# Attention plus MLP on one core: the last key tiles of the last set in two query halves, and three key tiles' values scaled in the first phase

## The chip, the core and the metric

The kernel runs on one core of a Trainium2 chip. The metric is device time in microseconds (us) of one execution, input and output transfers of the program included. Lower is better. In the texts TensorE is PE, ScalarE is ACT, VectorE is DVE, GpSimd is POOL and SyncE, which issues most of the DMAs, is SP.

## The reference

`x` has 2048 tokens of 512 features. After a layer norm, 32 heads of 16 features attend over all 2048 tokens; an MLP of width 1792 works on the same normalised tokens, normalised once more; both are added to `x`.

```python
x = A_x
xn = _layernorm(x, axis=-1)
return x + _A_ref(xn, A_wqkv, A_wo) + _B_ref(xn, B_w1, B_b1, B_w2, B_b2)
# _A_ref: q, k, v = split(x @ wqkv) into 32 heads of 16
#   p = softmax(q k^T * 16**-0.5);  return (p v) @ wo
# _B_ref: y = layernorm(x); h = gelu(y @ w1 + b1); return h @ w2 + b2
```

## The kernel before

**Tiling.** Queries come in 4 tiles of 512 (`QW`), heads in 8 sets of 4 (`HS`), keys in 16 tiles of 128. A set `g` (0 to 31, `g = 8 * query tile + head set`) has 16 key tiles times 4 heads = 64 units. A unit is one matmul of scores, 128 keys by 512 queries, into one of the 8 PSUM banks (`qk`, the matmul at L1054; four heads sit in four row groups of the array).

**Two ways to the exponential.** ACT takes most units: one instruction over 2 or 3 banks (`fex` in `build_tile`, L1237, 1024 or 1536 columns) writes weights into `p_sb`, which has 15 slots; a slot is free again after the value matmuls of its key tile (`pv`, L1072). DVE takes whole key tiles out of `KD` = (2, 5, 8, 11, 14) (`build_dve`, `dve_terms`): per head one conversion to int16 (L1319), then four adds per key tile (L1343) that make four shifted copies. Their bits, read as f16, are five terms of an approximated exponential, so such a key tile has five rounds of value matmuls, the last four with scaled copies of the values (`vs`). The denominators come from a column of ones in the values `va`. How many key tiles of `KD` go to DVE is settled while the order is made: a set whose other key tiles are used up gives the rest to ACT.

**Stages.** In the first phase sets 0 and 1 run while the tokens are normalised, transposed (`xnT`), and turned into keys (`kt`) and values (`va`). A value matmul for key tile k waits for the values of tile k and of tile k+1 (`deps` in `build_pv`). The key tiles in `VSE` get their four scaled copies straight from the PSUM bank of the value projection (`scaled`, L938); those of the others are made later from a projection that is done again. `XACT` says up to which group of four token tiles ACT copies half of the transposes out of PSUM. After that, sets 2 to 31 run one after the other, with the MLP (`build_mlp`, `build_down`) and the output projection (`build_out`) fitted in between.

**After a set.** `build_opost` copies the set's sums out of PSUM (`osb`, L1377), and takes the denominators through DRAM: save (`ldram`, L1379), load spread over the partitions (`lc`, L1381), reciprocal on DVE (L1384), save (`rdram`, L1386), broadcast to 128 partitions (`rlb`, 256 KB, L1389), product on DVE (L1391). All five DMAs are issued by SP, in one line with the loads of MLP weights (`w_r`) and tokens (`x_r`). There is one `rlb` buffer, so a broadcast waits for the product before it. For the last set `build_opost_last` does without DRAM: per half of the queries a transpose out of PSUM (L1418), reciprocal, product, transpose back, all on DVE. Then `build_final` multiplies by the last rows of `wo`, adds the sum kept so far (`acc`, by an fp32 matmul with an identity for output tiles 0 and 2, on DVE for 1 and 3) and stores.

**The order.** All engines run a fixed order, made when the program is built by a planner (`_Plan`): operations with assumed durations, dependencies and a priority (a due time) are placed one by one on the engine that is free first. `TOL` and `KEEP` say how far PE may prefer an operation of the kind it is at; `T0`, `NST`, `KG`, `HLO`, `DN0`, `OL0`, `RATE` and their like only shift due times, `RESL`, `OPEN` and `HOT` steer which operations may start. Where the plan finds PE without work it places fill matmuls of zeros (`fill`, L1630). On the chip every engine takes its instructions in this order, so one that waits holds up all behind it on its engine.

Of the kernel before, what the change touches and what calls it, by code (L numbers as in the profile page):

```python
# [11 lines left out]
ALU = mybir.AluOpType  # L12
# [10 lines left out]
P = 128  # L23
DH = 16
HS = 4
QW = 512
# [35 lines left out]
class _Plan:  # L62
# [9 lines left out]
    TOL = 0.075  # L72
    KEEP = 2.0
# [406 lines left out]
def kernel(  # L480
# [149 lines left out]
    T0, NST = 13.5, 11.75  # L630
    KG, R0, VSP, NFI = 16.0, 29.0, 500.0, 2
    OL0, OL1 = -0.35, 0.25
    PAIR1, EPR = 1, -15

    VSE = (5,)
    D1 = ((1, 8),)
    OUT0, OUT1 = 1.3, 0.3
    HLO, HHI, DN0, DN1 = 0.17, 0.36, 0.58, 0.11
    PAIR = 1
    VX = 3  # L640
    HLO0, HHI0 = 0.3, 0.12
    OUT, OPEN, RES, RESL, SLK, ALP = 3, 2, 36, 28, 55.0, 0.0
    KTP, QTP = 65.0, 85.0
    HOT = 2
    XACT = 2
    F2 = 300.0
    CHUNK = 4
    HOLD = 75.0
    RATE, QO, PO, AO, DO = 23.75, 50.0, 44.5, 40.0, 14.5
# [329 lines left out]
    n_a = {g: 0 for g in range(NG)}  # L979
    stream = {"u": 0, "g": 0, "tile": 0, "cur": None, "end": False}  # L980

    def take_unit():

        u = stream["u"]
        if u < NU2:
            stream["u"] = u + 1
            stream["g"] = 1 if u >= END0 else 0
            return first_units[u] + (T0 + (start[2] - T0) * u / NU2,)
        cur = stream["cur"]
        if not cur:  # L990
            g = max(stream["g"], 2)
            if not left_a[g] and not left_d[g]:
                if g == NG - 1:
                    stream["end"] = True
                    return None
                g += 1
            stream["g"] = g
            k = left_a[g].pop(0) if left_a[g] else left_d[g].pop()
            cur = stream["cur"] = [(g, k, j) for j in range(HS)]
        g, k, j = cur.pop(0)  # L1000
        n_a[g] += 1
        stream["u"] = u + 1
        return g, k, j, ts_(g, min(n_a[g] / (HS * 12), 1.0))

    def units_left(g):
        return HS * len(left_a[g]) + (len(stream["cur"] or ()) if stream["g"] == g else 0)
# [44 lines left out]
    def qk(bank, g, k, j):  # L1051
        qt, s = divmod(g, NS)
        lo = 32 * j
        I(nc.tensor.matmul(ps[:, bank, :], lhsT=kt[lo:lo + 32, s // 2, k * P:(k + 1) * P],  # L1054
                           rhs=qz[lo:lo + 32, (qt * NB + s // 2) % NQB, s % 2, :],
                           start=True, stop=True, tile_position=(lo, 0)))
# [6 lines left out]

    def pv(g, k, rows):

        qt, s = divmod(g, NS)
        for vals, wts in rows:
            pv_done[g] += 1
            end = g in all_built and pv_done[g] == pv_need[g]
            for j in range(HS):  # L1070
                h = 8 * (s // 2) + 2 * j + s % 2
                I(nc.tensor.matmul(ps[32 * j:32 * j + 32, o_bank[g], :], lhsT=vals[:, h * VS:h * VS + 32],  # L1072
                                   rhs=wts(j), start=pv_done[g] == 1, stop=end,
                                   tile_position=(0, 32 * j)))
        if g in o_open:
            o_open.remove(g)
        if not end:
            o_open.append(g)
# [120 lines left out]
    def build_tile():  # L1199
# [15 lines left out]
        def fqk():  # L1215
            dl_now[0] = dl
            for x, (g, k, j, _) in enumerate(us):
                qk(b0 + x, g, k, j)
            if i in rider:
                rides(i)  # L1220
            build_tile()
        deps = []
        for (g, k, j, _) in us:
            deps += qk_deps(g, k)
# [18 lines left out]
        for x, (g, k, j, _) in enumerate(us):  # L1243
            unit_exp[g, k, j] = e
            unit_slot[g, k, j] = s0 + x
            unit_seq[g, k, j] = seq0 + x
            if j == HS - 1:
                whole[g].append((k, us[0][3]))
                if len(whole[g]) == (PAIR if seq0 >= NU2 else PAIR1):
                    build_pv(g)  # L1250
# [5 lines left out]
    def whole_set(g):  # L1256
        if g not in all_built and not left_d[g] and (
                built[0] >= (END0, NU2)[g] if g < 2 else not left_a[g]
                and (g < stream["g"] or not stream["cur"])):
            finish(g)  # L1260

# [146 lines left out]
    def build_opost_last(g):  # L1408
# [4 lines left out]
        e0, e1, e2 = None, None, mk_ok  # L1413
        for hf in range(2):
            qs = slice(hf * QW // 2, (hf + 1) * QW // 2)
            cs = slice(hf * HC, (hf + 1) * HC)
            tav = ta[:, qs].rearrange("p (c r) -> p c r", r=32)
            e0 = add("DVE", 0.36, lambda qs=qs: I(nc.vector.transpose(  # L1418
                out=ta[:, qs], in_=ps[:, o_bank[g], qs])), pv_ops[g] + h_use + [e1], pr,
                rel=(o_done(g),) if hf else ())  # L1420

            def f1(qs=qs, cs=cs, tav=tav):
                I(nc.vector.reciprocal(out=rl_t[:, cs], in_=tav[:, :, DH]))
                I(nc.vector.tensor_tensor(out=on_t[:, cs], in0=tav,
                                          in1=rl_t[:, cs].unsqueeze(2).to_broadcast([P, HC, 32]),
                                          op=ALU.mult))
                I(nc.vector.transpose(out=ont[:, slot, qs],  # L1427
                                      in_=on_t[:, cs].rearrange("p c r -> p (c r)")))
            e1 = add("DVE", 0.95, f1, [e0] + list(ont_use.get(g - NON, ())), pr)
            on_last.append(e1)  # L1430

            def f2(cs=cs, tav=tav):
                I(nc.gpsimd.tensor_scalar(out=okl[:, 0, cs], in0=tav[:, :, DH], scalar1=L_MIN,
                                          scalar2=None, op0=ALU.is_ge))
                I(nc.gpsimd.tensor_scalar(out=okl[:, 1, cs], in0=tav[:, :, DH], scalar1=L_MAX,
                                          scalar2=None, op0=ALU.is_le))
                I(nc.gpsimd.tensor_tensor(out=okl[:, 0, cs], in0=okl[:, 0, cs], in1=okl[:, 1, cs],
                                          op=ALU.mult))
                I(nc.gpsimd.tensor_tensor(out=okall[:, cs], in0=okall[:, cs], in1=okl[:, 0, cs],
                                          op=ALU.mult))  # L1440
            e2 = add("POOL", 1.3, f2, [e0, e2], pr)
# [118 lines left out]
    def build_final():  # L1560
        ga, gb = NG - 2, NG - 1
        outs = []
        for c in range(TQ):
# [3 lines left out]
            pool = tailp if c else misc  # L1567
# [6 lines left out]
            def fa(key=key, c=c, cs=cs, pool=pool):  # L1574
                mm(ps[:, pool.bank(key), :], ont[:, ga % NON, cs],
                   wo_pad[:, (ga % NS) // 2, ga % 2, :], c % 2 == 1, False)
# [4 lines left out]
            acq = ((pool, key),) if c else ((one, key), (misc, key))  # L1581
            dep = [acc_op[c], mk_idf] + ([exp_prev[0]] if c else [])
            if c % 2 == 0:
# [5 lines left out]
            def fe(c=c, key=key, pool=pool):  # L1589
                if c % 2:  # L1590
# [4 lines left out]
            outs.append(add("DVE" if c % 2 else "ACT", dve(D), fe, [m, y_use[0]], pr,  # L1595
# [85 lines left out]
```

## Time and profile before

| | |
|---|---|
| four runs | 817.59, 817.98, 817.54, 814.90 us; median 817.57 |
| profiled execution | 817.47 us, span of its instructions 815.7 us, mean granted PE clock 0.995 |
| PE busy | 780.6 us (96%), 9887 matmuls |
| DVE busy | 751.3 us (92%) |
| ACT busy | 775.5 us (95%), of it 733.9 in 649 exponentials (L1237): 355 of 1024 columns at 1054 ns, 294 of 1536 at 1483 ns |
| DMA | 27.99 MB, mean 34 GB/s |

The span goes from the first to the last instruction; the profiled execution is 1.77 us longer than it. A line of the timeline gives the start, the length, the engine, the line of code, what is written from what, and in brackets the idle time of the engine before it with what ended it. Records of a matmul overlap those after it (0.39 us each; a group of four that share the array takes about 0.215 us from start to start).

### The profile page before, as it was taken

Reading aid. Unit: us, or ns where it says so; the run is one execution under the profiler, and the core shown is the slowest. Engines: PE = TensorE matmul, PEld = TensorE weight load, DVE = VectorE, ACT = ScalarE, POOL = GpSimd, SP = SyncE. Lnnn points to the kernel's source line nnn. Section 1 sums busy time; section 2 is a strip of 40 time slices with the busy share of each in tenths; the row PEclk is TensorE's granted clock in tenths of the full one; section 3 lists DMA queues with packets and bytes.
Section 4 is the critical chain, followed back from the end, with each engine's and each line's share of the span. In section 5 each row is a group of like instructions: output and inputs, shape, how many; then the busy total and the mean of one; then the engine's idle time right before and its main releaser. Section 6 shows DMA issues by size and latency. Waiting matters only on the chain. (4 is left out here: it accounts for less than half of the span.)

```text
span 815.7 us, 23268 instructions
## 1 busy us (share of the span) xinstructions
PE 780.6 (96%) x9887; PEld 260.8 (32%) x9888; DVE 751.3 (92%) x1304; ACT 775.5 (95%) x676; POOL 59.6 (7%) x165
## 2 busy tenths in 40 slices
PE   8899999999999999999999999899999999999997
PEld 3333332333332333333333333233332333333332
DVE  8959999997899999997999999799899999999885
ACT  6779999999999999999999999799999999999995
POOL 3300001001000000000000010000100110000001
PEclk9999999999999999999999999899999999999999
DMA  6300031101010011100002012100000101210000
GB/s 188 97 17 2 21 80 31 36 14 30 16 36 8 29 48 37 52 22 10 15 16 41 22 35 46 44 21 22 23 16 16 28 16 40 62 42 28 13 23 33
DMA packets 54798, 27.99 MB, mean 34 GB/s; under 512 B 40613, under 2 KB 50598, under 8 KB 54690
## 3 DMA queue, kind: packets, MB, share of 16 engines
q1 hardware_dynamic: 52818, 25.03, 11.3%
q8 instruction: 78, 1.28, 0.6%
q10 hardware_dynamic: 1872, 1.44, 0.6%
q14 instruction: 30, 0.25, 0.1%
HBM read 23.85 MB, written 2.61 MB: 32 GB/s over the span
## 5 line engine op out<-in xcount | busy, mean ns | idle before, releaser
L1237 ACT ACTIVATE p_sb<-ps 128x1024 bf16<-128x1024 f32 (+1 forms) x649 | 733.9, 1248 | 23.4 <-PE ps L1054 12.0
L1054 PE MATMUL ps<-qz,kt 32*128 32x512 bf16 x2048 | 311.7, 384 | 19.0 <-ACT p_sb L1237 6.5
L1319 DVE TENSOR_SCALAR x_sb<-ps 128x512 int16<-128x512 f32 x456 | 301.1, 680 | 22.3 <-PE ps L1054 20.7
L1343 DVE TENSOR_SCALAR tb_x<-x_sb 128x2048 int16<-128x2048 int16 x304 | 202.6, 680 | 1.8 <-PE ps L1072 1.2
L1054 PEld LDWEIGHTS <-kt 32*128 32x128 bf16 x2048 | 85.0, 91 | 276.9 <-issue 269.8
L1072 PE MATMUL ps<-p_sb,va 128*32 128x512 bf16 x1592 | 157.6, 390 | 0.3 <-DVE osb L1377 0.3
L1072 PE MATMUL ps<-tb_x,vs 128*32 128x512 f16 x1216 | 112.0, 383 | 1.1 <-DVE tb_x L1343 0.9
L1343 DVE TENSOR_SCALAR x_sb<-x_sb 128x2048 int16<-128x2048 int16 x152 | 103.5, 681 | 4.1 <-PE ps L1072 3.5
L1072 PEld LDWEIGHTS <-va 128*32 128x32 bf16 x2048 | 49.7, 93 | 107.6 <-issue 104.2
L1072 PEld LDWEIGHTS <-vs 128*32 128x32 bf16 x1824 | 50.4, 96 | 44.3 <-issue 23.9
L1398 POOL TENSOR_SCALAR okt<-lc 128x16 f32<-128x16 f32 x31 | 10.9, 352 | 701.8 <-DMA lc<-ldram 701.8
L597 PE MATMUL ps<-yT,w_r 128*32 128x512 bf16 x896 | 59.4, 385 | 1.6 <-DVE ht L1498 0.8
L1072 PE MATMUL ps<-x_sb,vs 128*32 128x512 f16 x608 | 59.8, 383 | 0.7 <-DVE x_sb L1343 0.6
L597 PE MATMUL ps<-w_sb,ht 128*32 128x512 bf16 x896 | 59.6, 380 | 0.0
L1072 PE MATMUL ps<-x_sb,va 128*32 128x512 f16 x456 | 45.0, 384 | 1.4 <-DVE x_sb L1319 1.2
L1498 DVE TENSOR_SCALAR ht<-ps,b_sb 128x512 bf16<-128x512 f32 x56 | 41.4, 739 | 2.3 <-PE ps L597 2.2
L1630 PE MATMUL ps<-ones_bf,zeros_bf 128*32 128x512 bf16 x416 | 36.8, 384 | 0.0
L597 PE MATMUL ps<-wo_pad,ont 128*32 128x512 bf16 x512 | 33.9, 380 | 0.5 <-DVE ont L1427 0.2
L597 PEld LDWEIGHTS <-w_r 128*32 128x32 bf16 x896 | 22.8, 96 | 26.1 <-issue 12.4
L597 PEld LDWEIGHTS <-ht 128*32 128x32 bf16 x896 | 21.7, 96 | 21.7 <-issue 5.7
L1508 ACT ACTIVATE ht<-ht 128x3584 bf16<-128x3584 bf16 x8 | 25.1, 3182 | 0.0
L1377 DVE COPY osb<-ps 128x512 f32<-128x512 f32 x31 | 21.1, 681 | 0.5 <-PE ps L1072 0.3
(100 smaller groups left out, 363.3 us busy)
## 6 DMA issues: line engine op xcount, KB each, us to landing
rlb<-rdram SPq DMA_DIRECT2D x31, 256.0 KB
w_r<-in_B_w_dram SPq DMA_DIRECT2D x56, 128.0 KB
x_r<-in_A_x_dram SPq DMA_DIRECT2D x16, 128.0 KB
w_sb<-in_B_w_dram SPq DMA_DIRECT2D x1, 1792.0 KB
out_dram<-ot SPq DMA_DIRECT2D x12, 128.0 KB
x_sb<-in_A_x_dram SPq DMA_DIRECT2D x2, 512.0 KB
wkv<-in_A_wqkv_dram ACTq DMA_DIRECT2D x1, 512.0 KB
x_sb<-in_A_x_dram ACTq DMA_DIRECT2D x1, 512.0 KB
```

The costliest lines, as they stand in the source:

```text
L597: I(nc.tensor.matmul(dst[32 * j:32 * j + 32], lhsT=lhsT[:, 32 * j:32 * j + 32], rhs=rhs, start=start, stop=stop, tile_position=(0, 32 * j)))
L1054: I(nc.tensor.matmul(ps[:, bank, :], lhsT=kt[lo:lo + 32, s // 2, k * P:(k + 1) * P], rhs=qz[lo:lo + 32, (qt * NB + s // 2) % NQB, s % 2, : ...
L1072: I(nc.tensor.matmul(ps[32 * j:32 * j + 32, o_bank[g], :], lhsT=vals[:, h * VS:h * VS + 32], rhs=wts(j), start=pv_done[g] == 1, stop=end, ...
L1237: I(nc.scalar.activation(p_sb[:, s0:s1, :].rearrange("p a b -> p (a b)"), ps[:, b0:b0 + n, :].rearrange("p a b -> p (a b)"), AF.Exp, scale ...
L1319: I(nc.vector.tensor_scalar(out=ib[sl][:, j, :], in0=ps[:, pool.bank(key), :], scalar1=LEVEL, scalar2=0.0, op0=ALU.add, op1=ALU.max))
L1343: I(nc.vector.tensor_scalar(out=tb[x].rearrange("p j q -> p (j q)"), in0=ib[sl].rearrange("p j q -> p (j q)"), scalar1=float(SHIFT[t]), sc ...
L1377: e0 = add("DVE", dve(QW), lambda: I(nc.vector.tensor_copy(osb[:, i2, :], ps[:, o_bank[g], :])), pvs + before, pr - 1000, rel=(o_done(g),))
L1398: I(nc.gpsimd.tensor_scalar(out=okt[:, 0, :], in0=lc[:, i2, :], scalar1=L_MIN, scalar2=None, op0=ALU.is_ge))
L1498: I(nc.vector.tensor_scalar(out=ht[:, fc, :], in0=ps[:, misc.bank(key), :], scalar1=b1_sb[:, fc:fc + 1], scalar2=None, op0=ALU.add))
L1508: I(nc.scalar.activation(out=hv, in_=hv, func=AF.Gelu_apprx_tanh, scale=1.0))
L1630: I(nc.tensor.matmul(ps[32 * j:32 * j + 32, o_bank[opened], :], lhsT=zeros_bf[:, 0:32], rhs=ones_bf[:], start=False, stop=False, tile_posi ...
```

## The change

1. **Last set in halves.** Of set 31, the last four key tiles that ACT takes (`NHK`), once DVE's key tiles are given out, are cut into half units: a unit now holds two key tiles for 256 queries. All half units of the first 256 queries come first, then those of the others. The first half goes into the set's bank, whose group is closed by a matmul of zeros; the second half goes into a bank of its own (`O2`), to which what the set's bank holds for these queries is added through a copy on DVE and an fp32 matmul with an identity.
2. **Post-processing by halves.** `build_last_half` does for one half what `build_opost_last` did in a loop, the first half as soon as its sums are complete. In `build_final` only output tile 2 takes `acc` by the fp32 matmul; tiles 0, 1 and 3 add it on DVE.
3. **Values.** `VSE` is (5, 8, 11) in place of (5,); `D1` is empty, so key tile 8 of set 1 goes to ACT; `XACT` is 3.
4. **Constants of the planner** are other ones, so the order changes everywhere.

```diff
-    TOL = 0.075
-    KEEP = 2.0
+    TOL = 0.05
+    KEEP = 1.0
...
-    T0, NST = 13.5, 11.75
-    KG, R0, VSP, NFI = 16.0, 29.0, 500.0, 2
-    OL0, OL1 = -0.35, 0.25
+    T0, NST = 14.0, 12.75
+    KG, R0, VSP, NFI = 14.75, 29.5, 450.0, 1
+    NHK = 4
+    OL0, OL1 = -0.95, 0.2
...
-    VSE = (5,)
-    D1 = ((1, 8),)
-    OUT0, OUT1 = 1.3, 0.3
-    HLO, HHI, DN0, DN1 = 0.17, 0.36, 0.58, 0.11
+    VSE = (5, 8, 11)
+    D1 = ()
+    OUT0, OUT1 = 1.075, 0.55
+    HLO, HHI, DN0, DN1 = 0.07, 0.42, 0.58, 0.05
     PAIR = 1
-    VX = 3
-    HLO0, HHI0 = 0.3, 0.12
-    OUT, OPEN, RES, RESL, SLK, ALP = 3, 2, 36, 28, 55.0, 0.0
-    KTP, QTP = 65.0, 85.0
-    HOT = 2
-    XACT = 2
-    F2 = 300.0
+    VX = 2
+    HLO0, HHI0 = 0.3, 0.135
+    OUT, OPEN, RES, RESL, SLK, ALP = 3, 2, 28, 30, 60.0, 25.0
+    KTP, QTP = 40.0, 85.0
+    HOT = 1
+    XACT = 3
+    F2 = 150.0
     CHUNK = 4
-    HOLD = 75.0
-    RATE, QO, PO, AO, DO = 23.75, 50.0, 44.5, 40.0, 14.5
+    HOLD = 0.0
+    RATE, QO, PO, AO, DO = 23.0, 70.0, 52.0, 32.5, 14.5
...
+            if g == NG - 1 and len(left_a[g]) <= NHK:
+
+                if not left_d[g]:
+                    halves.extend((ks, j, hf) for hf in range(2)
+                                  for ks in zip(left_a[g][::2], left_a[g][1::2])
+                                  for j in range(HS))
...
             dl_now[0] = dl
-            for x, (g, k, j, _) in enumerate(us):
-                qk(b0 + x, g, k, j)
+            for x, (g, k, j, _, *hf) in enumerate(us):
+                if not hf:
+                    qk(b0 + x, g, k, j)
+                for d in range(2 * len(hf)):
+                    qk(b0 + x, g, k[d], j, slice(d * QH, d * QH + QH),
+                       slice(hf[0] * QH, hf[0] * QH + QH))
...
+    def build_pv_half(g, ks, hf):
...
+            for d, k in enumerate(ks):
+                for j in range(HS):
+                    h = 8 * (s // 2) + 2 * j + s % 2
+                    I(nc.tensor.matmul(
+                        ps[32 * j:32 * j + 32, misc.bank("O2") if hf else o_bank[g], cs],
+                        lhsT=va[:, k, h * VS:h * VS + 32],
+                        rhs=p_sb[:, x[j][1], d * QH:d * QH + QH],
...
+            if not hf and complete(g):
+                for j in range(HS):
+                    I(nc.tensor.matmul(
+                        ps[32 * j:32 * j + 32, o_bank[g], :], lhsT=zeros_bf[:, 0:32],
+                        rhs=ones_bf[:], start=False, stop=True, tile_position=(0, 32 * j),
+                        skip_group_check=True))
...
+    def build_last_half(g, hf):
...
+        if hf == 0:
+            whole_o = pv_ops[g] + half_ops[0]
+            e0 = add("DVE", 0.45, lambda: I(nc.vector.transpose(
+                out=ta[:, qs], in_=ps[:, o_bank[g], qs])), whole_o + h_use, pr)
+            rest = slice(QH, QW)
+            c = add("DVE", 0.36, lambda: I(nc.vector.tensor_copy(
+                osb[:, g % 2, rest], ps[:, o_bank[g], rest])),
+                whole_o + [e0] + list(osb_use.get(g - 2, ())), pr, rel=(o_done(g),))
+
+            def fo():
+                half_left[1] -= 1
+                I(nc.tensor.matmul(ps[:, misc.bank("O2"), rest], lhsT=ident_f[:],
+                                   rhs=osb[:, g % 2, rest], start=False,
+                                   stop=half_left[1] == 0, skip_group_check=True))
+            half_ops[1].append(add("PE", 0.5, fo, [c, mk_idf], pr - 100, hold=1, mode="d"))
+        else:
+            e0 = add("DVE", 0.45, lambda: I(nc.vector.transpose(
+                out=ta[:, qs], in_=ps[:, misc.bank("O2"), qs])), half_ops[1] + [e1], pr,
+                rel=(misc.giver("O2"),))
...
-            pool = tailp if c else misc
+            pool = tailp if c > 1 else misc
...
-            if c % 2 == 0:
+            if c == 2:
                 dep = [add("PE", 0.9, fi, dep, pr - 20, acq=acq, mode="d")]
```

## The prediction

> **What bounds the kernel now.** First the busy shares of the page:
>
> ```profile
> PE 780.6 (96%) x9887; PEld 260.8 (32%) x9888; DVE 751.3 (92%) x1304; ACT 775.5 (95%) x676; POOL 59.6 (7%) x165
> ```
>
> PE and ACT look alike, so I asked for the waits of ACT by stretch. From 75 to 520 us it idles 4.3 us, from 540 to 804 us 1.6 us: there ACT is the bound, and what it is given or spared counts in full. Its other idle time lies in three places. In all:
>
> ```profile
> ACT p_sb L1237 <- PE ps L1054: 12.0, 30, 2.7
> ACT p_sb L1237 <- PE ps L1072: 8.0, 2, 4.5
> ```
>
> **Place one**, the first phase. The two waits for L1072 (value matmuls, which free slots of `p_sb`) are 3.48 us before 29.10 and 4.54 us before 49.32. ACT's timeline, then PE's:
>
> ```profile
> 41.01 3.77 ACT L1237 ACTIVATE p_sb<-ps 128x1024 bf16<-128x1024 f32 x4 [0.34 <-ACT p_sb L1237]
> 49.32 15.57 ACT L1237 ACTIVATE p_sb<-ps 128x1024 bf16<-128x1024 f32 x16 [4.54 <-PE ps L1072]
> ```
> ```profile
> 45.26 1.91 PE L597 MATMUL ps<-xnT,wkv 128*32 128x512 bf16 x32
> 47.10 1.91 PE L597 MATMUL ps<-wkv,xnT 128*32 128x512 bf16 x32
> 48.83 0.40 PE L1072 MATMUL ps<-p_sb,va 128*32 128x512 bf16 x4
> ```
>
> PE does 64 projection matmuls in one go before the value matmul (48.83) that frees the slots. That one needed the values of key tile 8, which DVE copies out at 48.20.
>
> **Place two**, 520 to 530 us. The windows (the column after POOL is the granted clock), the timeline, and the chain that ended last:
>
> ```profile
> 520.00:524.00 4.00, 1.90 (x23) 0.61 (x20) 1.75 (x4) 2.74 (x3) 1.30 (x4) 0.94 0.27 68
> 524.00:528.00 4.00, 3.92 (x33) 1.06 (x31) 3.31 (x6) 1.45 (x1) 0.00 (x0) 0.50 0.00 0
> 528.00:532.00 4.00, 4.00 (x49) 1.02 (x41) 2.70 (x5) 2.88 (x3) 0.00 (x0) 0.70 0.00 0
> ```
> ```profile
> 513.38 0.53 SPq L1389 DMA_DIRECT2D rlb<-rdram  x1
> 514.16 0.51 SPq L1379 DMA_DIRECT2D ldram<-osb  x1
> ...
> 522.25 0.25 DVE L1384 RECIPROCAL rc<-lc 128x16 f32<-128x16 f32 x1 [2.44 <-DMA lc<-ldram]
> ...
> 523.70 1.67 PE L1054 MATMUL ps<-qz,kt 32*128 32x512 bf16 x5 [2.10 <-DVE x_sb L1319]
> ...
> 525.48 1.45 ACT L1237 ACTIVATE p_sb<-ps 128x1536 bf16<-128x1536 f32 x1 [2.73 <-PE ps L1054]
> ```
> ```profile
> 514.16 4.50 DMA ldram<-osb
> 518.73 3.44 DMA lc<-ldram
> ```
>
> Set 18's broadcast of 256 KB goes out 0.78 us ahead of set 19's save. Save and load land after 8 us; in most sets POOL, which waits for the same load, starts 3.5 us after the copy. The reciprocal holds DVE for 2.44 us, PE runs dry for 2.10 us, its clock falls to half, and ACT loses 2.73 + 2.20 + 0.22 = 5.15 us.
>
> **Place three**, the tail. The last exponential ends at 805.41:
>
> ```profile
> 803.04 2.37 ACT L1237 ACTIVATE p_sb<-ps 128x1024 bf16<-128x1024 f32 x2 [0.23 <-PE ps L1054]
> ...
> 806.35 0.69 DVE L1553 TENSOR_TENSOR wkv<-ps,wkv 128x512 f32<-128x512 f32 x1 [1.47 <-PE ps L597]
> ...
> 806.96 0.44 DVE L1418 STREAM_TRANSPOSE ht<-ps 128x256 f32<-128x256 f32 x1
> ...
> 808.49 0.41 DVE L1418 STREAM_TRANSPOSE ht<-ps 128x256 f32<-128x256 f32 x1
> ...
> 810.13 0.62 PE L597 MATMUL ps<-wo_pad,ont 128*32 128x512 bf16 x8 [0.24 <-DVE ont L1427]
> ...
> 810.87 0.69 DVE L1591 TENSOR_TENSOR yT<-ps,wkv 128x512 bf16<-128x512 f32 x1
> ```
>
> Both halves' post-processing (1.59 us each) follows it in line; DVE ends at 811.56, 6.15 us after ACT. The 4.14 us from there to the end of the span are the store, the flag and the branch, which stay.
>
> **The change, part by part.** Counts are those of the built order; the sum is against the profiled execution, 817.47 us (0.10 under the median of the four runs).
>
> *More for ACT: +4.2 us.* Key tile 8 of set 1 goes to ACT (2 instructions of 1024 columns), and one more key tile does so in a later set (114 DVE key tiles become 112): 359 such instructions against 355, the 294 of 1536 stay. 4 x 1.05 = 4.2, on the path. The half units do not change ACT's columns. DVE loses 8 conversions and 8 adds, 16 x 0.68 = 11 us, and PE 10 - 2 = 8 rounds of value matmuls, 8 x 0.215 = 1.7 us: both have idle time already, so nothing.
>
> *First phase: -3.4 us.* Up to the score matmuls of unit 64, PE has 104 K and 176 V projection matmuls before, 40 and 192 after: 48 fewer, 12 groups of four x 0.215 = 2.6 us. Three groups of 16 transposes also come later (0.34 each, 1.0), and four changes between score and other matmuls go (0.32 from start to start for one group against 0.215, so 0.1 each, 0.4). PE is there 4.0 us earlier. The longest row of PE work without scores was 5.5 us here; after it is one projection (0.98) and one transposition. Key tile 8's copy stood behind four key copies, whose projections PE made first; now it follows that of tile 7 after two DVE instructions, and its projection is no longer late. The stall of 4.54 should go. Against it stand two PSUM copies that move to ACT (`XACT`; 2 x 0.588 = 1.18), in a stretch where PE and ACT are about level: I charge them in full, 4.54 - 1.18 = 3.4. Ends: 4.5 (copies hidden) and 1.2 (PE still late by half). The first stall has the same order of PE before it and stays. The eight scalings that come earlier (8 x 0.62 = 5.0 on DVE) fall where DVE has room: it is busy 11.2 us of the 20 from 40 to 60; without that cover they would cost 5.0. The two projections not made again (32 matmuls, 1.7 us of PE later on) are worth nothing where ACT is the bound.
>
> *Place two: -4.3 us.* All order changes, so this coincidence does too. In the new order, the DVE work between broadcast 18 and set 19's copy is 10.7 us; it was 0.6. If the event goes, ACT gets 5.15 us; at most the 1.6 us idle that ACT had later could have absorbed some of a delay, so 3.5 to 5.15; I take the middle. That the four runs hold one at 814.90, 2.6 below the others, fits a stall that does not always bite, but does not show it.
> The Trainium skill ("TensorE: Matmul & The Clock Gate", The HAM clock gate) has the clock fall after an idle window of about 3.4 us. Here 0.50 follows 2.10 us of idle, so the row decides. By the page's rule the loss would be the DVE wait alone, 2.4, and the forecast 814.0.
>
> *Tail: -1.9 us.* The first half's chain (1.59) and its carry into the second bank now stand before the last two half-unit value matmuls or beside them. From the last exponential: value matmuls 0.45 (0.06 to start, a group of 0.215, 0.17 to land), half two's chain 1.59, then on DVE three additions (0.65, 0.65, 0.69) and the reduction of 0.15 in line: 4.2 us against 6.15. PE's own line is shorter: 12 output matmuls 0.65, the fp32 identity 0.99 (1.98 for two in the trace), 16 more 0.86, ends at 3.0. Ends: 1.0, if the carry's fp32 matmul (256 columns, half of 0.99 = 0.5), which waits on DVE ahead of the last value matmuls in PE's line, comes late by a microsecond, or the last score matmuls, which stand behind twelve value matmuls of DVE's last terms, do; and 2.8, if only 0.45 + 1.59 + 0.62 + 0.69 = 3.35 counted.
> Score matmuls of 256 columns do not occur before; the nearest rows, 128 columns at 221 ns and 512 at 384, give for 16 more at most 16 x 0.38 = 6 us if each stood alone, and 0 if they share the array as their like do. PE has fills in this stretch, so I take 0.
> Against the change speaks "TensorEngine Tiling (Array Packing)", Instruction Overhead: some 60 cycles with each matmul. By that, the 32 more would cost an estimated 0.8 us of PE time, and the forecast would be 812.9.
>
> Sum: 4.2 - 3.4 - 4.3 - 1.9 = -5.4; 817.47 - 5.4 = **812.1 us**. With the ends of the terms taken partly together, 809.5 to 815.3. ACT's small waits elsewhere (5.9 us) may shift by 1 either way, inside that.
>
> **The rivals.** A difference of 0.3% (2.45 us, so 815.1 to 820.0) is about what a measurement here can tell.
>
> *One DMA wait takes the place of the old one: 816.4 to 817.3.* Counting DVE instructions at 0.61 us each (1.20 for two L1319 in the chain), a broadcast now goes out 0.6 to 1.8 us ahead of the next copy's end in six sets (1, 4, 5, 9, 24, 25), against two before (1 and 19, about 0.5). For it: number, and four loads of `wo` between set 4's save and load. Against: DVE work between copy and reciprocal is 6.1 us or more in five of them (4.8 in set 19, whose wait it was), and set 1, with a broadcast between save and load, had its data after 5.57 us, without a stall.
>
> *Two or more such waits, each with the clock drop: slower, 821.6 or more.* Same place; it decides once a load lands some 2 us after DVE has run out of work, as in set 19 (8.1 us). 812.1 + 4.3 + 5.15 = 821.6.
>
> *The first-phase saving fails: 816.6.* The added scalings hold one of the two PSUM banks of these projections for five DVE instructions each, and DVE is busy 19.46 us of the 20 from 20 to 40. If the stall comes back elsewhere, 812.1 + 4.54 = 816.6. Against: those of tile 8 come after the copies that the value matmuls wait for.
>
> **How the numbers follow.** Forecast 0.62 (nearly all under 815.1), one wait 0.17, no first-phase saving 0.10, two waits 0.11. Faster 0.61, same 0.27, slower 0.12. The range takes in the forecast's own 809.5 to 815.3 and the two middle cases with a microsecond above: 809 to 818.3; what it leaves out is the slower case and about 0.07 beside.
>
> **What would show it.** ACT without a stall of 4.5 us near 45 to 50, the one near 25 to 29 still there; 359 exponentials of 1024 columns; no window with a clock near 0.50 and no reciprocal with a wait over 1 us; DVE's last addition about 4.2 us after the last exponential, the first half's transpose before its end. Wrong, if ACT's idle time between 60 and 800 us grows beyond 8 us, if a reciprocal waits over 2 us for `lc`, or if the last exponential ends later than 804.

## The result, and the profile after

The changed kernel takes 818.91 us (median of 42 runs, 813.9 to 825.2 but for one disturbed run), the kernel before 816.72 (63 runs, 814.7 to 819.1): a ratio of 1.0028, 95% interval 1.0018 to 1.0039. The change makes the kernel slower by 0.28%, clear of noise but just under the 0.3% that the prediction took for what a measurement here can tell; it had forecast 812.1, a faster kernel. The profiled execution took 818.66 us, with a span of 816.9 and a mean granted clock of 0.990.

The busy shares and ACT's waits, from the page and the waits of the kernel after:

```profile
PE 776.5 (95%) x9823; PEld 257.6 (32%) x9824; DVE 741.8 (91%) x1288; ACT 779.5 (95%) x681; POOL 55.3 (7%) x165
```
```profile
ACT p_sb L1265 <- PE ps L1072: 13.3, 21, 6.1
ACT p_sb L1265 <- PE ps L1095: 4.3, 4, 3.8
```

PE and DVE have less to do, as predicted. ACT's longest wait is no longer one of 4.5 us for value matmuls (now L1095) but one of 6.1 us for score matmuls (now L1072). I added up ACT's time from the first to the last exponential in both traces, and what follows it:

| us | before | after | change | predicted |
|---|---|---|---|---|
| ACT busy | 770.1 | 774.7 | +4.6 | +4.2 + 1.2 |
| ACT idle up to 75 us | 9.7 | 4.9 | -4.8 | -4.5 |
| ACT idle behind 75 us | 13.9 | 16.0 | **+2.1** | **-4.3** |
| last exponential to DVE's end | 6.21 | 4.07 | -2.1 | -1.9 |
| DVE's end to the end of the span | 4.06 | 5.45 | **+1.4** | **0** |

Three of the five rows came as predicted; the two others turn -5.4 into +1.2.

**First phase.** ACT's timeline of the kernel after:

```profile
29.12 2.87 ACT L1265 ACTIVATE p_sb<-ps 128x1024 bf16<-128x1024 f32 x3 [3.77 <-PE ps L1095]
...
37.08 23.15 ACT L1265 ACTIVATE p_sb<-ps 128x1024 bf16<-128x1024 f32 x24
```

The first stall stands, the second, at 49 us, is gone: 24 exponentials follow one another.

**The new wait.** SyncE's issues around set 4's save, then the timeline of all engines, ACT's timeline, and the windows (the eighth figure of a window, after POOL's, is the granted clock):

```profile
149.66 0.82 SPq L665 DMA_DIRECT2D wo_pad<-in_A_wo_dram  x2
150.57 0.55 SPq L1468 DMA_DIRECT2D rlb<-rdram  x1
151.17 0.96 SPq L665 DMA_DIRECT2D wo_pad<-in_A_wo_dram  x2
152.18 0.51 SPq L1458 DMA_DIRECT2D ldram<-osb  x1
152.75 2.69 SPq L665 DMA_DIRECT2D wo_pad<-in_A_wo_dram  x4
159.85 0.36 SPq L1460 DMA_DIRECT2D lc<-ldram  x1
```
```profile
161.84 0.25 DVE L1463 RECIPROCAL rc<-lc 128x16 f32<-128x16 f32 x1 [3.52 <-DMA lc<-ldram]
...
162.70 0.58 PE L1072 MATMUL ps<-qz,kt 32*128 32x512 bf16 x1 [3.40 <-DVE x_sb L1398]
```
```profile
173.55 7.31 ACT L1265 ACTIVATE p_sb<-ps 128x1024 bf16<-128x1024 f32 x6 [6.12 <-PE ps L1072]
```
```profile
160.00:164.00 4.00, 1.30 (x6) 0.21 (x5) 2.15 (x5) 3.98 (x3) 0.92 (x4) 0.72 0.05 6
164.00:168.00 4.00, 4.00 (x27) 0.90 (x30) 2.97 (x5) 3.42 (x3) 0.00 (x0) 0.50 0.00 0
```

The broadcast of 256 KB (`rlb`) and eight loads of `wo` lie around the save, four of them between it and its load. SyncE waits until 159.85 for the save to land, 7.7 us after its issue. The reciprocal holds DVE for 3.52 us, PE runs dry for 3.40, the clock falls to half for 10.2 us, and ACT, which has other work until 167.4, loses 6.12 us before 173.55. This is place two of the kernel before again, larger, in set 4 instead of 19.

**The end.** The timeline of all engines, cut to DVE:

```profile
805.92 0.45 DVE L1502 STREAM_TRANSPOSE ht<-ps 128x256 f32<-128x256 f32 x1 [0.57 <-PE ps L1095]
...
807.88 0.45 DVE L1516 STREAM_TRANSPOSE ht<-ps 128x256 f32<-128x256 f32 x1 [0.16 <-PE ps L1314]
...
811.27 0.13 DVE L1552 CAST flag_i<-ps 1x1 int32<-1x1 f32 x1
```

The first half is transposed 1.4 us before the last exponential ends (807.34), and DVE ends 4.07 us behind it, as predicted. Then comes what no view of the profile lists, since branches do not count as busy; the trace has it. All engines read the flag and branch past the code that is not needed. PE's branch takes 3.28 us (812.53 to 815.81; before 0.41), one of SyncE's last waits stands behind it from 814.57 to 815.96, and the span ends 1.4 us later after DVE's end than before.

### The profile page after: what moved, and what is told of

Its sections match the earlier page's. It is cut to its first block, busy times and chain, and to the rows that moved or that the text cites. A ratio compares the mean times of both kernels' runs of the same rounds, so it can differ in the third digit from the quotient of the medians.

```text
span 816.9 us, 23106 instructions
## 1 busy us (share of the span) xinstructions
PE 776.5 (95%) x9823; PEld 257.6 (32%) x9824; DVE 741.8 (91%) x1288; ACT 779.5 (95%) x681; POOL 55.3 (7%) x165
## 4 chain that ended last, share of the span: by engine, by line
PE 29%; DVE 22%; ACT 8%; issue 4%; DMA 2%; DVEq 0%; SPq 0%; ACTq 0%
PE ps L1095 10%; DVE x_sb L1398 10%; PE ps L597 9%; PE ps L1072 9%; ACT p_sb L1265 7%; DVE tb_x L1422 5%; DVE x_sb L1422 3%; DMA ldram<-osb 1%; DVE ht L1601 1%; ACT ht L1611 1%; DVE osb L1456 1%; DMA lc<-ldram 1%; DVE qc L919 0%; DVE ont L1470 0%; PE ps L1733 0%
## 5 line engine op out<-in xcount | busy, mean ns | idle before, releaser
L1072 PE MATMUL ps<-qz,kt 32*128 32x512 bf16 (+1 forms) x2064 | 310.9, 381 | 21.4 <-DVE x_sb L1398 9.2
L1398 DVE TENSOR_SCALAR x_sb<-ps 128x512 int16<-128x512 f32 x448 | 296.1, 680 | 28.8 <-PE ps L1072 28.1
L1422 DVE TENSOR_SCALAR tb_x<-x_sb 128x2048 int16<-128x2048 int16 x299 | 199.4, 681 | 5.1 <-PE ps L1095 4.0
L1072 PEld LDWEIGHTS <-kt 32*128 32x128 bf16 x2064 | 83.4, 91 | 269.8 <-issue 262.6
L1095 PE MATMUL ps<-p_sb,va 128*32 128x512 bf16 x1584 | 157.5, 390 | 0.9 <-DVE x_sb L1398 0.7
L1095 PE MATMUL ps<-tb_x,vs 128*32 128x512 f16 x1196 | 110.8, 384 | 2.3 <-DVE tb_x L1422 1.8
L1422 DVE TENSOR_SCALAR x_sb<-x_sb 128x2048 int16<-128x2048 int16 x149 | 101.5, 681 | 1.9 <-PE ps L1095 1.6
L1095 PEld LDWEIGHTS <-va 128*32 128x32 bf16 x2032 | 48.5, 93 | 105.2 <-issue 102.6
L1095 PEld LDWEIGHTS <-vs 128*32 128x32 bf16 x1792 | 50.8, 96 | 52.4 <-issue 31.3
L1477 POOL TENSOR_SCALAR okt<-lc 128x16 f32<-128x16 f32 x31 | 14.5, 468 | 707.1 <-DMA lc<-ldram 707.1
L1095 PE MATMUL ps<-x_sb,vs 128*32 128x512 f16 x596 | 58.7, 383 | 1.5 <-DVE x_sb L1422 1.3
L1095 PE MATMUL ps<-x_sb,va 128*32 128x512 f16 x448 | 44.2, 384 | 0.9 <-DVE kt L901 0.5
L597 PEld LDWEIGHTS <-w_r 128*32 128x32 bf16 x896 | 21.7, 96 | 23.9 <-issue 10.2
```

What stands on the lines that cost most here:

```text
L597: I(nc.tensor.matmul(dst[32 * j:32 * j + 32], lhsT=lhsT[:, 32 * j:32 * j + 32], rhs=rhs, start=start, stop=stop, tile_position=(0, 32 * j)))
L1072: I(nc.tensor.matmul(ps[:, bank, to], lhsT=kt[lo:lo + 32, s // 2, k * P:(k + 1) * P], rhs=qz[lo:lo + 32, (qt * NB + s // 2) % NQB, s % 2, of],
L1398: I(nc.vector.tensor_scalar(out=ib[sl][:, j, :], in0=ps[:, pool.bank(key), :], scalar1=LEVEL, scalar2=0.0, op0=ALU.add, op1=ALU.max))
L1422: I(nc.vector.tensor_scalar(out=tb[x].rearrange("p j q -> p (j q)"), in0=ib[sl].rearrange("p j q -> p (j q)"), scalar1=float(SHIFT[t]), sc ...
L1477: I(nc.gpsimd.tensor_scalar(out=okt[:, 0, :], in0=lc[:, i2, :], scalar1=L_MIN, scalar2=None, op0=ALU.is_ge))
```

## The experiments

Theory: the wait of set 4, by its DMAs, costs what place two was to give, and the constants, which set the order, bring it. Rivals: the halves cost something, or the clock does by itself. Times of the kernel before lie beside each run on the same chip; ratios are to it.

**1. The halves alone.** The new code with the constants of the kernel before:

```diff
...
-    OL0, OL1 = -0.95, 0.2
+    OL0, OL1 = -0.35, 0.25
...
-    VSE = (5, 8, 11)
-    D1 = ()
+    VSE = (5,)
+    D1 = ((1, 8),)
...
```

> The new code with the planner's constants, VSE, D1 and XACT of before: the order is that of before up to the last key tiles. Theory (the tail gain is real, the loss is a late load): last exponential to DVE's end 4.1 us instead of 6.2, time about 2 us under before (814.7), set 19's wait still there in about as many executions as before. Rival (the half units cost as much as they bring): within 0.7 us of before.

Measured 817.47 us, ratio 1.0016 (1.0005 to 1.0027). The gain did not come: it is 1.0 us over the kernel before on the same chip, slower than theory and rival had it. In its timeline DVE's last sum of the output projection is late, and the first half's transpose behind it:

```profile
805.64 0.69 DVE L1656 TENSOR_TENSOR wkv<-ps,wkv 128x512 f32<-128x512 f32 x1 [2.10 <-PE ps L597]
806.25 0.44 DVE L1502 STREAM_TRANSPOSE ht<-ps 128x256 f32<-128x256 f32 x1
```

That is 1.7 us after the last exponential (804.58), and DVE ends 7.25 us after it. The halves need the new due times, which have this work done earlier.

**2. The constants alone.** The code before with all the constants of the kernel after.

```diff
...
-    VSE = (5,)
+    VSE = (5, 8, 11)
...
-    RATE, QO, PO, AO, DO = 23.75, 50.0, 44.5, 40.0, 14.5
+    RATE, QO, PO, AO, DO = 23.0, 70.0, 52.0, 32.5, 14.5
...
```

> The code of before with all constants of the change (VSE, D1 and XACT among them): the order is that of the changed kernel up to the last key tiles. Theory: the whole loss is here, 820.5 to 821.5 us (the changed kernel's 818.9 plus the 2 us of the tail), set 4's load lands about 10 us after the copy, PE idles over 3 us behind it and its clock falls to 0.5. Rival (the halves or their added bank hold PE up earlier): not slower than before by more than 1 us.

Measured 817.34 us, ratio 1.0017 (1.0001 to 1.0032), three to four under the expectation: I had taken the event at its full price. By its time alone (0.9 us over the kernel before) the rival came in; the trace decides between them. The event is there: the reciprocal of set 4 waits 3.05 us, PE idles 2.93, and the half clock begins at 161.6. It comes with the constants. They also bring the first phase's gain (idle 5.0 us up to 75) and 0.7 us of the tail (5.53 us after the last exponential; before 6.21). What the kernel after has beyond this one, 1.5 us less in the tail and 1.4 us more behind DVE's end, nearly cancels.

**3. The loads of `wo` later.** The kernel after, with the eight loads issued behind set 5's broadcast; nothing else moves on any engine.

```diff
...
+        def f_rlb():
+            I(nc.sync.dma_start(rlb[:], bcast(rdram[i2])))
+            if g == 5:
+                for f in wo_late:
+                    f()
-        e3 = add("SP", 0.5, lambda: I(nc.sync.dma_start(rlb[:], bcast(rdram[i2]))),
+        e3 = add("SP", 0.5, f_rlb,
...
```

> The changed kernel; only SP's order differs: the eight loads of wo, which stood around set 3's broadcast and between set 4's save and load, are issued behind set 5's broadcast. Theory (those loads delay set 4's denominators): no wait of the reciprocal over 1.5 us, no half clock near 162 us, ACT's 6.1 us wait gone, median 5 to 6 us under the changed kernel, 813 to 814, and a narrower spread. Rival (the new order starves ACT whatever the loads do): median above 817.

Measured 812.8 us, ratio 0.9956 (0.994 to 0.9971), 6 us under the kernel after. Set 4's wait is gone: `lc` is issued 3.0 us after the save, where it took 7.7.

```profile
152.34 0.50 SPq L1460 DMA_DIRECT2D ldram<-osb  x1
155.38 0.34 SPq L1462 DMA_DIRECT2D lc<-ldram  x1
```

The eight loads were the cause, together with the broadcast (run 6 has them without it). Two of the eight runs took 816.86 and 816.95 us; the first is the profiled one, in which the clock falls to half at 608.8 for 13.7 us (see runs 13 and 14).

**4. And two broadcast buffers.** As 3, with an `rlb` for each of two sets, so that a broadcast does not wait for the product before it and goes out away from the next save. (A small tile shares the space of another to make room.)

```diff
-    rlb = const.tile([P, QW], F32, name="rlb")
+    rlb = const.tile([P, 2, QW], F32, name="rlb")
...
-            I(nc.sync.dma_start(rlb[:], bcast(rdram[i2])))
+            I(nc.sync.dma_start(rlb[:, i2, :], bcast(rdram[i2])))
```

> As the run before, and the broadcast has two buffers (the small tile r2b shares the space of rt for it): no broadcast waits for the product of the set before, so none goes out just ahead of a save; the order on each engine stays. Theory: set 9's wait of 1.1 us goes as well, all saves land within 2 us of their issue, median 812 to 813, clock 0.995 or more in all executions. Rival (collisions under 2 us cost nothing): no difference to the run before within 0.5 us.

Measured 810.95 us, ratio 0.9932 (0.9915 to 0.995), 1.9 us under run 3, whose interval overlaps with this one. No reciprocal waits any more, `lc` goes out 1.8 us after the save, and ACT idles 7.9 us behind 75 us instead of 16.0. ACT's waits, against those of the kernel after:

```profile
ACT p_sb L1267 <- PE ps L1074: 5.1, 18, 0.6
ACT p_sb L1267 <- PE ps L1097: 4.5, 4, 4.0
```

**5. The kernel before with two broadcast buffers.** The diff of 4 on the kernel before.

> The kernel before with two buffers for the broadcast (r2b shares the space of rt), the order of each engine as before: set 18's broadcast no longer waits and goes out long ahead of set 19's save. Theory (this coincidence is the price that the prediction took for place two): no wait of set 19's reciprocal, no half clock at 524 us, median 2 to 4 us under before. Rival (ACT makes it up elsewhere): within 0.7 us of before.

Measured 813.37 us, ratio 0.997 (0.9958 to 0.9983), 3.3 us under the kernel before on the same chip; the prediction had 4.3 for place two, with ends at 3.5 and 5.15. Between the two profiled executions it is 4.4 us (817.47 to 813.09). The stall differs from execution to execution: set 19's reciprocal waits 2.44 us in the profile of the kernel before, 1.94 in run 1's, 1.81 in run 6's and 0.71 in run 11's.

**6. The eight loads in set 6 of the kernel before,** between save and load, far from a broadcast.

```diff
+        def f_ld():
+            I(nc.sync.dma_start(ldram[i2], osb[DH:P:32, i2, :]))
+            if g == 6:
+                for f in wo_late:
+                    f()
...
```

> The kernel before; only SP's order differs: the eight loads of wo are issued right behind set 6's save, ahead of its load. Theory (loads between save and load hold up the reciprocal): set 6's reciprocal waits 2 us or more, PE idles behind it, the clock falls, median 3 to 6 us over before. Rival (the loads are small and land in time): within 0.7 us of before.

Measured 816.95 us, ratio 1.0009 (0.9996 to 1.0021): nothing lost, the theory's 3 to 6 us missed. SyncE's issues, DVE's timeline and a window:

```profile
210.31 0.53 SPq L1382 DMA_DIRECT2D ldram<-osb  x1
210.89 3.71 SPq L814 DMA_DIRECT2D wo_pad<-in_A_wo_dram  x8
214.70 0.36 SPq L1388 DMA_DIRECT2D lc<-ldram  x1
```
```profile
217.87 0.25 DVE L1391 RECIPROCAL rc<-lc 128x16 f32<-128x16 f32 x1 [2.08 <-DMA lc<-ldram]
```
```profile
216.00:220.00 4.00, 4.00 (x60) 1.17 (x50) 2.13 (x5) 4.00 (x5) 0.90 (x4) 1.00 0.06 7
```

`lc` goes out 4.4 us after the save, as soon as the loads are issued, and DVE waits 2.08 us. But PE is busy throughout at full clock, and ACT too. So with the loads alone the save lands in 4.4 us or less, against 7.7 with the broadcast too, and this wait of DVE cost nothing, since PE had other matmuls in line.

**7. Fills for PE in the wait.** The kernel after, with 14 more groups of matmuls of zeros ahead of the score matmul that waits at 162.70.

```diff
+        def f_rc():
+            I(nc.vector.reciprocal(rc[:, i2, :], lc[:, i2, :]))
+            I.extra = 14 if g == 4 else I.extra
...
```

> The changed kernel with 14 more groups of fill matmuls (3.0 us at full clock) on PE ahead of the score matmul that waits for DVE in set 4; nothing else moves. Theory (most of the price is the clock, not the wait): the reciprocal still waits over 2 us, but no half clock near 162 us, ACT's wait at 173 us falls from 6.1 to under 2, median 3 to 5 us under the changed kernel's 818.9. Rival (the price is the wait itself): ACT's wait stays over 4 us, median 818 or more.

Measured 817.06 us, ratio 1.0019 (1.0003 to 1.0034), 1.85 under the kernel after: short of what was expected, and PE's branch, at 0.41 us here, has some of it (runs 9 to 11). ACT's timeline, and the window that answers to 160 to 164 above:

```profile
170.41 9.93 ACT L1268 ACTIVATE p_sb<-ps 128x1024 bf16<-128x1024 f32 x8 [2.57 <-PE ps L1075]
```
```profile
160.00:164.00 4.00, 4.00 (x59) 1.36 (x51) 2.74 (x6) 4.00 (x2) 0.91 (x4) 1.00 0.06 8
```

The clock stays up, and ACT's loss falls from 6.12 to 2.57 us. In this profile, though, half clock comes at 655.1 for 10.2 us, after a wait of 0.74 us of set 24's reciprocal and with no time over 0.7 us in which PE was idle. ACT idles 4.0 us there, between 655.8 and 666.3: what was won at 173 us went there. The time of this execution thus does not show the 3.5 us that the trace shows at the place itself.

**8. Without the halves.** The code before with the constants of the kernel after, the loads of `wo` later and two broadcast buffers: beside run 4 it leaves out the halves alone.

> The code of before with the change's constants, the eight loads of wo behind set 5's broadcast, and two broadcast buffers: against e4 only the halves are missing. Theory (the halves bring what the tail showed, 5.5 us from the last exponential to DVE's end without and 4.1 with): 1.5 us over e4, 812.5. Rival (the halves bring nothing, as with the constants of before): within 0.5 us of e4's 810.95.

Measured 811.35 us, ratio 0.9941 (0.9925 to 0.9958): by its time, 0.4 us over run 4, this is the rival's outcome. But DVE ends 5.53 us after the last exponential, against 4.07 in run 4, so the halves do save 1.5 us there. The spans are 809.3 and 809.1 all the same. From DVE's end to the end it takes 4.03 us here and 5.92 in run 4, whose branch of PE takes 3.91 us (0.41 here). Hence runs 9 to 11.

**9, 10, 11. PE's branch.** Each of the first eight fills, in which PE only waits for the tokens, is cut into eight pieces (nine in 11). That lengthens PE's code and moves the branch; its place is counted here in blocks of 256 of PE's instructions. The order stays.

```diff
+                    cut = [0, 64, 128, 192, 256, 320, 384, 448, 512] if n_cold[0] < 8 else [0, 512]
...
+                    for c0, c1 in zip(cut, cut[1:]):
+                        r = I(nc.tensor.matmul(ps[:, OB, c0:c1], lhsT=zeros_bf[:], rhs=ones_bf[:, c0:c1],
...
```

> The kernel after, in which each of the first eight fill matmuls of zeros (512 columns, before 6.5 us, while PE waits for the tokens) is cut into eight of 64 columns. That puts 112 more instructions into PE's code ahead of the branch at its end and changes nothing else in the order. In the profile after, PE's branch past the code that is not needed takes 3.28 us, and SyncE waits for it; in the profile before it takes 0.41 us. Theory: what the branch takes goes by where it lies in the 256 instructions (16 KB) of code that are fetched at a time; here it moves from 198 to 54, as in the seventh run, where it took 0.41. Branch 0.41 us, 4.1 us from DVE's end to the end of the span instead of 5.45, and a median about 1.4 us under the 818.9 of the kernel after. Rival: the branch is late because PE's own last work is, in the changed ending: still 3 us or more, and no difference in the median beyond 0.5 us.

> The fourth run's kernel (the loads of wo later, two rlb buffers) with the same 112 more instructions at the start of PE's code. Its branch took 3.91 us, and DVE's end to the end of the span 5.92 us. Theory: branch 0.41, 4.1 us behind DVE's end, median 1.8 under 810.95, so about 809.1. That would also be what the halves save at the end beside the eighth run's 811.35, which has them not. Rival: still 3.9 us, median within 0.5 us of 810.95.

> The reverse: the kernel before, in which each of the first eight fills is cut into nine pieces of 56 or 64 columns, 128 more instructions in PE's code. The branch moves from 70 to 198 within its 256 instructions, which is where it lies in the kernel after. Theory: its branch takes 3 to 4 us instead of 0.41, SyncE waits for it, and the median rises 1.4 to 1.9 us over that of the kernel before. Rival: only the new ending makes the branch slow: 0.41 us, and no change beyond 0.5 us.

| | kernel | PE's branch, us | DVE's end to end, us | median | ratio (95%) |
|---|---|---|---|---|---|
| 9 | after | 3.28 to 0.41 | 5.45 to 4.09 | 818.41 | 1.0025 (1.0009 to 1.004) |
| 10 | run 4 | 3.91 to 0.41 | 5.92 to 4.08 | 810.18 | 0.9926 (0.9909 to 0.9943) |
| 11 | before | 0.41 to 4.25 | 4.06 to 6.08 | 816.69 | 1.0008 (0.9993 to 1.0023) |

The branch follows its place in the code in both directions, and what stands behind it does too: 1.4, 1.8 and 2.0 us. The medians moved by 0.5, 0.8 and 0.2 us only. In the profiles of 9 and 11 PE waits 0.8 and 1.0 us for the load of `wq_sb` at 16 us, and 11's place two was mild (the reciprocal waits 0.71 us). So the branch's price is shown by the trace, and the medians, which other changes of this size overlay, do not confirm it by themselves.

**12. One scaled tile.** The kernel after with `VSE` as before.

```diff
-    VSE = (5, 8, 11)
+    VSE = (5,)
```

> The kernel after with one key tile's values scaled in the first phase (VSE = (5,)) as before, all its other constants kept. In the built order of this kernel the long row of projections ahead of the value matmuls near 45 us is gone too. Theory: the stall of 4.54 us goes by the planner's constants (fewer value projections ahead of unit 64), not by which tiles are scaled: ACT's idle time up to 75 us stays at about 5 us, with one stall of 3.5 to 4 us. Rival, the reason that the prediction gave (tile 8's projection and copy move forward because it is scaled there): a second stall of about 4.5 us near 45 to 50 us is back, 9 us of idle time in all.

One run, 824.69 us; what it has over the kernel after lies in the end (10.2 us from the last exponential to DVE's end, against 4.07). ACT idles 6.3 us up to 75, between the two expectations (5 and 9), and its timeline has no second stall:

```profile
41.44 26.86 ACT L1265 ACTIVATE p_sb<-ps 128x1024 bf16<-128x1024 f32 x28 [0.16 <-PE ps L1072]
```

The stall of 4.54 us went by the planner's constants, not by which tiles are scaled. That it is the fewer projections ahead of unit 64 in their order is argued; no run changes these alone.

**13, 14. The stretches in which the array is used least.** Of the 43 runs of the kernel after up to 825.2 us (the profiled one included), the 19 with a mean clock of 0.988 or less took 819.6 us or more, the other 24 took 819.5 or less, with a median of 816.9. The 19 are called the second group here, though the times pass from one to the other without a gap. The profiles so far have half clock in odd places; the windows of run 10:

```profile
606.00:610.00 4.00, 3.54 (x31) 1.06 (x29) 3.89 (x7) 3.98 (x4) 0.00 (x0) 1.00 0.24 41
610.00:614.00 4.00, 4.00 (x29) 0.82 (x26) 3.81 (x7) 2.99 (x3) 0.00 (x0) 0.53 0.00 0
614.00:618.00 4.00, 4.00 (x30) 0.75 (x27) 2.16 (x4) 2.47 (x2) 0.00 (x0) 0.50 0.03 6
```

PE counts as busy for 3.54 of 4 us before the clock falls, but with 31 matmuls, each on a quarter of the array. In each trace, the half-clock stretches all begin, within 2 ns, on one grid of 3.413 us, whose position differs from execution to execution. I worked out for every window of the grid how much of the array was in use (rows and columns in use times columns streamed, as a share of all; this is worked out from the matmuls' records, each counted from its start, and no view lists it):

```
use in the window | half clock follows | not
0.00 to 0.364     | 15                 | 0
0.365 to 0.372    | 0                  | 6
0.373             | 1                  | 0
0.374 and more    | 0                  | all the others
```

These are the windows at full clock from 18 to 795 us in the 16 profiles of this case; the line was drawn before runs 13 and 14, and two of the 15 are of run 13. Counting each matmul 0.06 us later moves the figures near the line by up to 0.015, so it is known to about that. The length of a stretch follows the same count, though no run was made to test this: of the 34 windows at half clock, the 18 with up to 0.376 of the array's full-clock capacity in use were followed by another, the 16 with 0.382 or more by full clock. Runs 13 (on the kernel after) and 14 (on that of run 4) put 22 groups of fills behind value matmuls where the use is lowest:

```diff
+            n_pv[1] += n_pv[0] in LOW
+            if n_pv[1] and not end:
+                n_pv[1] -= 1
+                for j in range(HS):
+                    I(nc.tensor.matmul(ps[32 * j:32 * j + 32, o_bank[g], :], lhsT=zeros_bf[:, 0:32],
+                                       rhs=ones_bf[:], start=False, stop=False, ...
```

> The kernel after with 22 more groups of fill matmuls of zeros (0.215 us each), put behind value matmuls in the stretches where the array is used least (near 48, 83, 105, 157, 235, 288, 371, 407, 605 to 615, 657, 740 and 746 us). In the profiles so far all half-clock stretches of one execution begin on one grid of 3.41 us, and each follows a grid window in which the array was used under about 0.365 of full (rows and columns in use times columns streamed); the grid lies differently in each execution. Theory: with the fills no such window is left but that of set 4's wait, so the second group of runs goes: nearly all runs at a mean clock of 0.990 or more, spread about 3 us, median 815 to 816.5 (816.5 of the lower group, less 1.4 for PE's branch, which these 176 instructions move to 118 of 256, plus up to 1 for the fills). Rival: the clock drops for another reason (at random, by power): about half of the runs still at 0.978 to 0.988 and 819 to 824 us, median 817 or more.

> The fourth run's kernel (loads of wo later, two rlb buffers) with the same 22 fills; PE's branch lies at 118 of 256 here too. Theory: no window under 0.365 is left at all; all runs at a clock of 0.997 or more, none over 812, branch 0.41 us, median 808.5 to 809.8. Rival: the fills cost more than they save, 810.2 (the tenth run) or more, and single runs at 815 or 816 with a clock of 0.985 to 0.99 remain.

Run 13: 817.51 us, ratio 0.9997 (0.9986 to 1.0009), against 1.0028 for the kernel after: 2.5 us less, of which the branch (0.41 us here) has 1.4 by the traces; beside run 9, whose branch is short too, it is 2.3 us less. Of 12 runs none has a clock under 0.989 or takes over 819.2 us: the second group is gone. One forecast failed: besides set 4's wait, a second half clock is left in its profile, at 659.7 for 3.4 us, after a wait of 1.66 us of set 24's reciprocal. The median is 1 us over what was expected; the kernel before ran at 817.64 on this chip, 0.9 over its median elsewhere. Run 14: 809.73 us, ratio 0.9903 (0.9887 to 0.9919), four runs within 0.2 us at a clock of 0.998 or more, as expected. It has the lowest median of all, 7.9 us under the kernel before on the same chip, and is faster than both kernels.

## Why the prediction was wrong

**More for ACT, +4.2:** right. 359 and 294 exponentials as counted; with the two copies ACT is busy 4.6 us longer, where 5.4 were charged.

**First phase, -3.4:** right in size (idle -4.8, of which the two copies take 1.2 back), by luck in part: of the reason given, the scaling of tile 8 does not matter (run 12), and that fewer projections ahead of unit 64 did it fits runs 2 and 12 but was not shown alone.

**Place two, -4.3: this step failed.** Its size was about right for the execution that the sum started from (4.4 by the profiles of run 5, 3.3 by the medians); the median of all runs of the kernel before, 816.72, already lies 0.75 under that execution. What failed is "if the event goes": it held for set 19 only. ACT's idle time behind 75 us, which was to fall by 4.3 us, rose by 2.1: the new wait alone costs 6.12 us. The rival of one wait in its place had the place, set 4, and the cause, loads of `wo` between save and load; I gave it 0.17, because DVE has 6.1 us of work or more between copy and reciprocal there and a load was late by 8.1 us at most. Here the load landed 9.8 us after the copy, and DVE had run out of work 6.3 us after it: 3.5 us of wait. The eight loads (run 3) turned a collision that DVE's work covered into one that it did not. The rule "some 2 us after DVE has run out of work" held here, though not in run 6, where 2.08 us cost nothing; the landing time had been taken from a set without such loads.

The step also took the clock for a matter of that one wait. By the table, what counts is how much of the array is used in a window of 3.41 us. The new order has six stretches at 0.34 to 0.36 (near 105, 155, 233, 612, 656 and 745 us) in which the clock can fall if the grid lies so; before, two at 0.36 (204 and 645). Hence, as run 13 shows, the runs up to 825 us, and a median of 818.9 where the calmer 24 have 816.9. The profiled execution has one of them, at 236.8, worth 1.4 us of ACT's idle time. "TensorE: Matmul & The Clock Gate" of the Trainium skill (The HAM clock gate) says that the window is free-running, 4096 cycles or 3413 ns, and does not start anew with a kernel; the grid in these traces, 3.413 us and elsewhere in each execution, agrees. It also has the throttle come after an idle window; here the windows at 233.4 us (kernel after) and 606.8 us (run 10), with 0.35 of the array in use, were followed by half clock, so the measurement decides against that reading.

**Tail, -1.9:** right as far as it was costed, -2.1 to DVE's end; the 256-column matmuls cost ACT nothing, as taken. "The store, the flag and the branch, which stay" was wrong: they grew by 1.4 us, because PE's branch lies elsewhere in its code. The Trainium skill ("Runtime: NRT & Kernel Launch", Instruction fetch mechanics) says that a taken branch whose target is not among the pages at hand must fetch it first. A branch of 0.41 us or of 3.3 to 4.3, by where it lies, fits that; which place is bad (198 of 256 was; 54, 70, 102, 118 and 133 were not) stands on no page and was not mapped here.

**What would show it wrong** was named: a reciprocal that waits over 2 us for `lc` (3.52), a last exponential later than 804 (807.34), and idle time of ACT beyond 8 us between 60 and 800 us (16.0). The range (809.0 to 818.3) missed by 0.6 us, since it had room for one wait, not for one that is larger than the old one, a slow branch and runs of lower clock besides. Left open: why the window at 0.373 was followed by half clock and the six from 0.365 to 0.372 were not, which may be no more than the uncertainty of the count.

## What to carry to other kernels

When an order is made anew, price each DMA that is waited for by what is queued around it in the new order, not by the landing times of the old one, and count how long the waiting engine's work lasts beyond it. Look through the order for stretches in which PE is "busy" with few matmuls on a quarter of the array, and fill them: here 22 groups of zeros took the spread of runs from 11 us (43 runs) to 4 (12 runs), and to 0.2 (4 runs) once the waits were gone, where it had been 3.5 (6 runs of run 4). And end a comparison at the last instruction of the program, not at the last engine's work.

## What the runs showed of the hardware

- Half clock begins on a grid of 3.413 us that is fixed within an execution, and lasts one to four of its windows (3.4 to 13.7 us). Under 0.365 of the array in use it followed in 15 of 15 windows, and over it in one; it ended after a window with 0.382 or more, in 16 of 16, and after none with 0.376 or less, of 18. The time follows the mean clock, 813.9 us at 0.996 and 825.2 at 0.978 for the same program.
- A save of 8 KB lands so that its reader can be issued 1.8 us after it (run 4), 3.0 with a broadcast of 256 KB issued 1.9 us ahead of it (run 3), 4.6 with it issued 0.8 us ahead (set 19 of the kernel before), and 7.7 with that broadcast and eight loads of 64 KB around it (kernel after).
- PE's branch at the end of the program took 0.41 us or 3.3 to 4.3 us by its place in PE's code, and the end of the span followed by 1.4 to 2.0 us.
